# Chunked attention before two layers: heads taken two pairs at a time, one attention cluster in every second slot

## The chip, the cores and the metric

The kernel runs on one core of a Trainium2 chip. The metric is device microseconds of one execution. TensorE (PE) multiplies, VectorE (DVE), ScalarE (ACT) and GpSimd (POOL) do the elementwise work, SyncE (SP) and POOL issue the DMAs. PSUM, where PE writes, is cut here into four tiles of 128x2x512: bank_x, bank_w, bank_y and bank_z.

## The reference, cut to what matters

```python
# q, k, v: (8, 8, 576, 64), in chunks of 64 rows
scores = (1 / np.sqrt(64)) * q_c @ k_c.T              # per head and chunk, 64x64
scores = scores - scores.max(-1, keepdims=True)
attn = np.exp(scores); attn = attn / (attn.sum(-1, keepdims=True) + 1e-9)
x = heads_side_by_side(attn @ v_c)                    # (4608, 512)
h = x @ w_in                                          # 2048 wide
g = np.where(h > 0, h, np.exp(np.minimum(h, 0)) - 1)  # ELU
y = g @ w_out
out = (sigmoid(y @ w_gate) * (y @ w_val)) @ w_out2
```

## The kernel before, in words

Everything is recorded by hand in one order (`manual_schedule`); each engine executes its instructions in that order, and semaphores make it wait for the others. Stage 1 does attention and the first layer, stage 2 the product with w_out, stages 3 and 4 the gated layer and the last product. A large product is three fp32r matmuls ("passes") per pair of 128x128 weights and 512 tokens: high with high, low with high, high with low. So weights and x are split in a high half (a cast on ACT) and a low half (a subtraction on DVE or POOL).

The unit of attention is a pair `A` of heads over 256 tokens, 72 of them. Its steps are `scores` (8 matmuls of 64x64, L463, each two records in the trace), `softmax_max` (DVE, L487 and L488), `softmax_exp` (ACT, L492), `softmax_sum` (DVE L497 and L498; the product L499 on POOL, later on DVE), `transposes` (PE, L505), `transposes_out` (ACT, L514), `values` (8 matmuls, L463) and `values_out` (ACT, L527) into a tile `xr`. When two pairs have filled a tile of 512 tokens, `x_high` (ACT, L380) and `x_low` (DVE, L384) split it. Scores, transposes and values of all pairs lie in bank_x (in `first_steps` in bank_x and bank_z by turns).

The first layer has 72 slots `d`: nine blocks of 512 tokens with eight slots each. A slot's 24 matmuls (`layer_in`, L395) fill one of bank_w, bank_y, bank_z by turns, for two tiles `n` of weights. `elu_exp`, `elu_rest` (ACT, L410, L413) and `elu_sum` (DVE, L418) read that bank in the next slot and store to DRAM. Each slot from 0 to 62 also holds on PE the values of pair d+9, the scores of d+11 and the transposes of d+10, next to one another ahead of the layer's matmuls (in slots 0 to 7 the transposes stand between the halves of the layer).

Before slot 0, `first_steps` takes 11 pairs through the same steps and does parts of the layers of slots 0 and 1. `bg(n)` lets n steps of a background list run: first `convert_in` (w_in from float64 bits; eight units of four steps on ACT, DVE and POOL, 1 MB of load each, two buffers), three steps a slot up to slot 6; then `convert_pairs` for the other weights, about four steps a slot. `join` of unit n issues the load of unit n+2; `rest` of unit n must have run before the layer of slot n.

In stages 3 and 4, `get` and `free` hand out ten buffers; `finish` of a unit multiplies by the gate, stores `s` and `t` to DRAM and frees both.

Of the kernel before, what the change touches and what calls it, by code (L numbers as in the profile page):

```python
# [8 lines left out]
F32 = mybir.dt.float32  # L9
# [16 lines left out]
PB = NPAIR // NB  # L26
KC = DM // 128
# [8 lines left out]
LEAD = 11  # L36
# [3 lines left out]
PRE_STEPS = (0, 0, 0, 1, 1, 1, 1, 1, 1, 1, 1, 2, 2)  # L40
W_AT = (3, 6)
# [19 lines left out]
def kernel(  # L61
# [287 lines left out]
    def shaped(t, shape):  # L349
        n = 1  # L350
        for k in shape:
            n *= k
        names = " ".join("abc"[:len(shape)])
        return t[:, 0:n].rearrange(f"p ({names}) -> p {names}", **dict(zip("abc", shape)))
# [14 lines left out]
    def stage_1():  # L369

        xr, xs, raws, vals, st, h_done = {}, {}, {}, {}, {}, {}

        def xr_tile(j, kk):
            if (j, kk) not in xr:
                xr[j, kk] = x_r.tile([128, TB], F32, tag=f"xr{kk}", name=f"xr{kk}")
            return xr[j, kk]

        def x_high(j, kk):
            x = xs[j, kk] = (x_l, x_r)[j % 2].tile([128, 2, TB], F32R, tag=f"xs{kk}", name=f"xs{kk}")
            nc.scalar.copy(out=x[:, 0], in_=xr[j, kk])  # L380

        def x_low(j, kk):
            x = xs[j, kk]
            nc.vector.tensor_sub(out=x[:, 1], in0=xr.pop((j, kk)), in1=x[:, 0])  # L384
# [46 lines left out]
        with (  # L431
# [5 lines left out]
            def with_eps(t):  # L437
                t = t.rearrange("p (n k) -> p n k", n=4)
                nc.gpsimd.memset(t[:, :, CH:], EPS)
                return t  # L440

            e4 = with_eps(c_p.tile([128, 272], F32, name="e4")[:, 0:4 * (CH + 1)])

            def load_raw(A):
                if A < NPAIR:
                    raws[A] = a_p.tile([128, 2, 4, CH], F32, tag="raw", name="raw", bufs=2)
                    nc.sync.dma_start(out=raws[A], in_=qkv[A][:, 0:512])

            def load_values(A):
                if A < NPAIR:  # L450
                    vals[A] = a_p.tile([128, 4, CH], F32, tag="vals", name="vals", bufs=2)
                    nc.sync.dma_start(out=vals[A], in_=qkv[A][:, 512:768])

            def small(tag):
                return a_p.tile([128, 16], F32, tag=tag, name=tag)[:, 0:4].rearrange("p (n k) -> p n k", k=1)
# [16 lines left out]
            def parts(ps, o):  # L472
                return ps[:, :, o:o + 128].rearrange("p g (i k) -> p i g k", i=2)

            def scores(A, ps):
                r = raws.pop(A)
                st[A, "ps"] = ps
                products(ps, 128, r[:, 0], r[:, 1])
                if A >= LEAD:
                    load_raw(A + 2)  # L480

            def softmax_max(A):
                if A not in st:
                    st[A] = [a_p.tile([128, 4, CH], F32, tag=k, name=k) for k in "sp"] + [e4, None]
                ps, s, m = parts(st.pop((A, "ps")), 128), st[A][0], small("m")
                s, m = (t.rearrange("p (i g) k -> p i g k", g=2) for t in (s, m))
                nc.vector.tensor_reduce(out=m[:, :, :, 0], in_=ps, op=ALU.max, axis=AX.X)  # L487
                nc.vector.tensor_tensor(out=s, in0=ps, in1=m.to_broadcast([128, 2, 2, CH]), op=ALU.subtract)  # L488

            def softmax_exp(A):  # L490
                s, _, e, _ = st[A]
                nc.scalar.activation(out=e[:, :, 0:CH], in_=s, func=ACTF.Exp, scale=SCALE)  # L492

            def softmax_sum(A, eng):
                _, p, e, _ = st[A]
                d = small("d")
                nc.vector.tensor_reduce(out=d[:, :, 0], in_=e, op=ALU.add, axis=AX.X)  # L497
                nc.vector.reciprocal(out=d, in_=d)  # L498
                eng.tensor_tensor(out=p, in0=e[:, :, 0:CH], in1=d.to_broadcast([128, 4, CH]), op=ALU.mult)  # L499

            def transposes(A, ps):
                p = st[A][1]
                st[A, "ps"] = ps
                for i in range(2):
                    nc.tensor.transpose(  # L505
                        ps[:, 0, 256 + 128 * i:384 + 128 * i],
                        p[:, 2 * i:2 * i + 2].rearrange("p n k -> p (n k)"), ident,
                    )

            def transposes_out(A):  # L510
                t = st[A][3]
                if t is None:
                    t = st[A][3] = a_p.tile([128, 4, CH], F32, tag="t", name="t")
                nc.scalar.copy(out=t.rearrange("p n q -> p (n q)"), in_=st.pop((A, "ps"))[:, 0, 256:512])  # L514

            def values(A, ps):
                t = st.pop(A)[3]
                st[A, "ps"] = ps
                products(ps, 0, vals.pop(A), t)
                if A >= LEAD:  # L520
                    load_values(A + 2)

            def values_out(A):
                j, i = divmod(A, PB)
                hp, c = divmod(i, 2)
                x = xr_tile(j, hp)[:, 256 * c:256 * c + 256]
                nc.scalar.copy(  # L527
                    out=x.rearrange("p (i g q) -> p i g q", i=2, g=2), in_=parts(st.pop((A, "ps")), 0),
                )
                return (j, hp) if c == 1 else None  # L530

            def first_steps(load_w):

                for A in range(LEAD):
                    t = w_p.tile([128, 1024], F32, tag="w", name="qkv0")
                    nc.sync.dma_start(out=t[:, 0:512], in_=qkv[A][:, 0:512])
                    nc.sync.dma_start(out=t[:, 512:768], in_=qkv[A][:, 512:768])
                    t = t[:, 0:768].rearrange("p (m n k) -> p m n k", m=3, n=4)
                    raws[A], vals[A] = t[:, 0:2], t[:, 2]
                    if A in W_AT:  # L540
                        load_w(W_AT.index(A))
                for A in range(LEAD):
                    t = w_p.tile([128, 1024], F32, tag="w", name="work")
                    s, p = (t[:, o:o + 256].rearrange("p (n k) -> p n k", n=4) for o in (0, 256))
                    st[A] = [s, p, with_eps(t[:, 512:772]), s]
                for A in (LEAD, LEAD + 1):
                    load_raw(A)
                    load_values(A)
                lows = []
                for k in range(PB + 5):  # L550
                    ps = bank["xz"[k % 2]]
                    n = k - 3
                    if 0 <= n < LEAD - 1:
                        transposes(n, ps)
                    if k < LEAD:
                        scores(k, ps)
                    n = k - 4
                    if 0 <= n < PB + 1:
                        values(n, ps)
                    for d in range(EARLY):  # L560
                        if 2 * d + 1 in w1:
                            layer_in(d, min((k - 5) // 2, KC))
                    for x in lows:
                        x_low(*x)
                    lows = []
                    if 0 <= k - 1 < LEAD:
                        softmax_exp(k - 1)
                    if 0 <= k - 2 < LEAD:
                        softmax_sum(k - 2, nc.gpsimd)
                    steps = PRE_STEPS[k] if k < len(PRE_STEPS) else 0  # L570
                    bg(steps // 2)
                    if k < LEAD:
                        softmax_max(k)
                    if 0 <= k - 3 < LEAD - 1:
                        transposes_out(k - 3)
                    if 0 <= k - 4 < PB + 1:
                        x = values_out(k - 4)
                        if x is not None:
                            x_high(*x)
                            lows.append(x)  # L580
                    bg((steps + 1) // 2)
                for x in lows:
                    x_low(*x)

            def slot(d, steps):

                c = LEAD + d
                ps = bank["x"]
                q = [steps // 3 + (i < steps % 3) for i in range(3)]
                if c - 2 < NPAIR:  # L590
                    values(c - 2, ps)
                if c < NPAIR:
                    scores(c, ps)
                if d < HF:
                    layer_in(d, KC, (0,))
                if c - 1 < NPAIR:
                    transposes(c - 1, ps)
                layer_in(d, KC, (1,) if d < HF else (0, 1))
# [487 lines left out]
```

## Time and profile before

| | |
|---|---|
| median of three runs | 1637.91 us (1636.05 to 1639.51) |
| the profiled execution | 1638.73 us, of which the span from first to last instruction is 1636.9 us |
| granted TensorE clock, mean | 0.997 of full speed |
| PE busy | 1602.9 us, 98% of the span |
| DVE, ACT, POOL busy | 1200.1, 749.1, 303.8 us |
| DMA | 423.19 MB, mean 259 GB/s |

Busy times are unions over a stretch; an engine can wait inside an instruction's gap without it being seen in them. In a row of the timeline an entry in brackets is the idle time ahead of the instruction and what ended it. PE's records overlap, since a matmul starts while the one before it drains; the distance between starts is what one costs.

### The profile page before, as it was taken

What the parts mean: (1) busy time and instruction counts of PE and PEld (TensorE: products, weight loads), DVE (VectorE), ACT (ScalarE), POOL (GpSimd) and SP (SyncE); (2) the same over time, 40 slices, a digit from 0 to 9 for tenths busy, and PEclk for the clock granted to TensorE, in tenths of its full rate; (3) what the DMA queues carried; (4) which work ended last, traced back from release to release, by engine and by line L of the source; (5) the groups of instructions that cost most, each with busy time, mean ns of one, the idle gap of its engine ahead of it and who ended that gap; (6) DMA issues with size and microseconds to landing.
All of it is one profiled execution on the core that took longest, in us unless ns stands there. A gap on an engine that the chain in (4) does not pass through costs nothing.

```text
span 1636.9 us, 25299 instructions
## 1 busy us (share of the span) xinstructions
PE 1602.9 (98%) x9636; PEld 1330.7 (81%) x9636; DVE 1200.1 (73%) x1662; ACT 749.1 (46%) x1244; POOL 303.8 (19%) x491
## 2 busy tenths in 40 slices
PE   6899999999999999999999999999999998999999
PEld 4677777777788898888888888888889887888888
DVE  6878888888637679988865676676675446777775
ACT  5767667766644455554442233332332123344342
POOL 3431111112101112222121223212211113000000
PEclk9999999999999999999999999999999999999999
DMA  6668888888887779999699769869565679433331
GB/s 229 206 216 293 296 293 290 278 288 291 280 292 257 224 297 390 378 336 410 210 302 322 251 208 385 303 222 407 180 206 174 216 261 391 180 141 140 144 103 52
DMA packets 157192, 423.19 MB, mean 259 GB/s; under 512 B 13840, under 2 KB 31248, under 8 KB 149904
## 3 DMA queue, kind: packets, MB, share of 16 engines
q0 software_dynamic: 71760, 218.13, 40.0%
q1 hardware_dynamic: 85312, 203.45, 35.7%
q8 instruction: 76, 1.25, 0.3%
q14 instruction: 44, 0.36, 0.1%
HBM read 288.88 MB, written 132.64 MB: 258 GB/s over the span
## 4 chain that ended last, share of the span: by engine, by line
PE 75%; DVE 12%; ACT 8%; issue 2%; DMA 2%; POOL 0%; SPq 0%; ACTq 0%; DVEq 0%; POOLq 0%
PE bank_z L747 11%; PE bank_y L747 11%; PE bank_x L747 10%; PE bank_x L902 9%; PE bank_y L902 9%; PE bank_z L902 9%; PE bank_w L747 5%; PE bank_w L902 5%; DVE elu L418 2%; PE bank_z L395 2%; PE bank_y L395 2%; PE bank_w L395 2%; DVE s L488 1%; ACT elu L413 1%; DVE m L487 1%
## 5 line engine op out<-in xcount | busy, mean ns | idle before, releaser
L95 ACT CAST four<-b 128x512 fp32r<-128x512 f32 (+1 forms) x240 | 128.0, 577 | 79.1 <-PE bank_z L747 20.9
L101 DVE TENSOR_TENSOR four<-b,four 128x512 fp32r<-128x512 f32 (+1 forms) x240 | 140.0, 631 | 30.5 <-ACT four L95 30.4
L902 PE MATMUL bank_z<-four,w 128*128 128x512 f32 (+1 forms) x720 | 157.6, 368 | 0.0
L924 ACT ACTIVATE s<-s 128x512 f32<-128x512 f32 (+1 forms) x60 | 35.4, 590 | 250.0 <-DVE s L104 250.0
L902 PEld LDWEIGHTS bank_z<-four,w 128*128 128x128 f32 x720 | 126.3, 189 | 22.5
L337 POOL DMA_DIRECT2D w<-wd_glu x159 | 86.1, 545 | 301.7 <-PE bank_x L902 115.1
L395 PE MATMUL bank_w<-xs,w 128*128 128x512 f32 x576 | 139.8, 397 | 0.0
L395 PE MATMUL bank_y<-xs,w 128*128 128x512 f32 x576 | 138.1, 394 | 1.4 <-POOL w L167 0.9
L395 PE MATMUL bank_z<-xs,w 128*128 128x512 f32 x576 | 138.8, 397 | 0.0
L395 PEld LDWEIGHTS bank_z<-xs,w 128*128 128x128 f32 x576 | 107.6, 190 | 21.7
L395 PEld LDWEIGHTS bank_y<-xs,w 128*128 128x128 f32 x576 | 106.2, 188 | 23.1 <-POOL w L167 1.2
L395 PEld LDWEIGHTS bank_w<-xs,w 128*128 128x128 f32 x576 | 106.9, 189 | 21.7
L337 POOL DMA_DIRECT2D w<-wd_mid x105 | 56.0, 537 | 265.8 <-PE bank_x L747 83.1
L747 PE MATMUL bank_x<-four,w 128*128 128x512 f32 (+1 forms) x480 | 100.2, 368 | 0.0
L747 PE MATMUL bank_y<-four,w 128*128 128x512 f32 (+1 forms) x480 | 100.2, 368 | 0.0
L747 PE MATMUL bank_z<-four,w 128*128 128x512 f32 (+1 forms) x480 | 100.2, 368 | 0.0
L747 PEld LDWEIGHTS bank_x<-four,w 128*128 128x128 f32 x480 | 83.7, 189 | 15.0
L747 PEld LDWEIGHTS bank_y<-four,w 128*128 128x128 f32 x480 | 83.7, 189 | 15.0
L747 PEld LDWEIGHTS bank_z<-four,w 128*128 128x128 f32 x480 | 83.7, 189 | 15.0
L104 DVE TENSOR_TENSOR s<-bank_z,s 128x1024 f32<-128x1024 f32 (+1 forms) x60 | 66.9, 1115 | 36.2 <-PE bank_z L902 35.1
L902 PE MATMUL bank_y<-four,w 128*128 128x512 f32 (+1 forms) x432 | 88.5, 354 | 0.1
L902 PE MATMUL bank_x<-four,w 128*128 128x512 f32 (+1 forms) x432 | 88.4, 354 | 0.0
(145 smaller groups left out, 3144.0 us busy)
## 6 DMA issues: line engine op xcount, KB each, us to landing
w<-wd_glu POOLq DMA_DIRECT2D x159, 512.0 KB, 7.9
w<-wd_mid POOLq DMA_DIRECT2D x105, 512.0 KB, 8.2
gd<-elu SPq DMA_DIRECT2D x72, 512.0 KB, 3.9
b<-gd SPq DMA_DIRECT2D x32, 1024.0 KB, 9.0
wd_glu<-ch POOLq DMA_DIRECT2D x36, 512.0 KB, 5.1
b<-gv SPq DMA_DIRECT2D x16, 1024.0 KB, 5.2
raw<-in_qkv SPq DMA_DIRECT2D x61, 256.0 KB, 4.0
wd_mid<-ch POOLq DMA_DIRECT2D x24, 512.0 KB, 5.0
```

Of the source, the lines that this page charges most:

```text
L95: nc.scalar.copy(out=out, in_=raw)
L101: lo_eng.tensor_sub(out=lo, in0=raw, in1=hi)
L104: nc.vector.tensor_tensor(out=out, in0=a, in1=b, op=ALU.add)
L337: nc.gpsimd.dma_start(out=t, in_=wd[m][q][:, LEFT[i]])
L395: nc.tensor.matmul(out=h_bank(d)[:, n], lhsT=w[:, zw, kk * 128:(kk + 1) * 128], rhs=xs[j, kk][:, zx], start=(kk == 0 and p == 0), stop=(kk ...
L413: nc.scalar.activation(out=elu[d], in_=elu[d], func=ACTF.Relu, scale=-1.0, bias=1.0)
L418: nc.vector.scalar_tensor_tensor(out=e, in0=h_bank(d), scalar=0.0, in1=e, op0=ALU.max, op1=ALU.subtract,)
L487: nc.vector.tensor_reduce(out=m[:, :, :, 0], in_=ps, op=ALU.max, axis=AX.X)
L488: nc.vector.tensor_tensor(out=s, in0=ps, in1=m.to_broadcast([128, 2, 2, CH]), op=ALU.subtract)
L747: nc.tensor.matmul(out=bank[PRODUCTS[i]][:, u, 0:NLS[j]], lhsT=w[:, k, zw, 128 * u:128 * u + 128], rhs=t[k][:, zx], start=(i < 4 and p == ...
L902: nc.tensor.matmul(out=ps[:, b], lhsT=w[:, b, zw, 128 * k:128 * k + 128], rhs=x_part(j, i, zx, k), start=(i < 4 and k == 0 and p == 0), st ...
L924: nc.scalar.activation(out=x, in_=x if of is None else of, func=ACTF.Sigmoid)
```

## The change

The unit becomes a group `G` of two pairs (36 of them), and `LEAD` goes from 11 pairs to 6 groups. Softmax instructions take eight heads' chunks (128x512) in place of four (128x256), a group's two exp tiles are shared by all groups, and p is written over s. A slot with even d holds the values of group d/2+4, the scores of d/2+6 and the transposes of d/2+5, between the two halves of the layer; a slot with odd d holds only its layer on PE, and `softmax_sum` on DVE. The transposes go to the second half of the bank that the next slot's layer will sum in (`h_bank(d + 1)[:, 1]`), so they wait for `elu_sum(d - 2)`, and the layer of slot d+1 waits for `transposes_out`. `values_out` and `xr` are gone: `x_high` and `x_low` read bank_x. `elu_rest` follows `elu_exp` at once. `first_steps` has six iterations and twelve background steps as before; each now waits for its own exp. In stage 4 the two buffers of the last unit are freed three products later.

```diff
-LEAD = 11
+LEAD = 6
-PRE_STEPS = (0, 0, 0, 1, 1, 1, 1, 1, 1, 1, 1, 2, 2)
+PRE_STEPS = (0, 1, 2, 3, 3, 3)
+        def x_high(j, kk, ps):
+            xs[j, kk] = (x_l, x_r)[j % 2].tile([128, 2, TB], F32R, tag=f"xs{kk}", name=f"xs{kk}")
+            nc.scalar.copy(out=half(j, kk, 0), in_=parts(ps, 0))
+        def x_low(j, kk, ps):
+            nc.vector.tensor_sub(out=half(j, kk, 1), in0=parts(ps, 0), in1=half(j, kk, 0))
...
+                for k in range(LEAD):
+                    scores(k, own(k))
+                    if k >= 2:
+                        values(k - 2, own(k))
+                    if k >= 1:
+                        transposes(k - 1, own(k - 1)[:, :, 256:512])
...
+                layer_in(d, KC, (0,))
+                if even:
+                    if G - 2 < NG:
+                        values(G - 2, ps)
+                    if G < NG:
+                        scores(G, ps)
+                    if G - 1 < NG:
+                        transposes(G - 1, (
+                            own(G - 1)[:, :, 256:512] if d == 0 else
+                            h_bank(d + 1)[:, 1].rearrange("p (g n) -> p g n", g=2)
+                        ))
+                layer_in(d, KC, (1,))
                 if d > 0:
                     elu_exp(d - 1)
+                    elu_rest(d - 1)
                 bg(q[0])
+                if even:
+                    if d > 0:
+                        elu_sum(d - 1)
+                    if G < NG:
+                        softmax_max(G)
+                    if G - 1 < NG:
+                        transposes_out(G - 1)
+                    if G - 2 < NG:
+                        x_high(*x_of(G - 2), ps)
+                    if G < NG:
+                        softmax_exp(G)
+                    bg(q[1])
+                    if G - 2 < NG:
+                        x_low(*x_of(G - 2), ps)
+                else:
+                    if G < NG:
+                        softmax_sum(G, nc.gpsimd if d < HF - 1 else nc.vector)
                     elu_sum(d - 1)
+                    bg(q[1])
...
-                    while pending:
-                        pending.pop(0)()
+                    if pending:
+                        done = pending.pop(0)()
+                    elif j == i == 0 and p == QO - 1:
+                        for x in done:
+                            free(x)
```

PE in slot 9 of before, from the cluster to the next one (bank_w is this slot's layer, the xs tiles are block 1's four quarters of x):

```order
L463 MATMUL bank_x<-t,vals 64x64 x8
L463 MATMUL bank_x<-raw 64x64 x8
L505 MATMUL bank_x<-ident,p 128x128 x2
L395 MATMUL bank_w<-xs_625,w 128x512 x3
L395 MATMUL bank_w<-xs_760,w 128x512 x3
L395 MATMUL bank_w<-xs_912,w 128x512 x3
L395 MATMUL bank_w<-xs_1063,w 128x512 x3
L395 MATMUL bank_w<-xs_625,w 128x512 x3
L395 MATMUL bank_w<-xs_760,w 128x512 x3
L395 MATMUL bank_w<-xs_912,w 128x512 x3
L395 MATMUL bank_w<-xs_1063,w 128x512 x3
L463 MATMUL bank_x<-t,vals 64x64 x8
```

PE in slot 8 of the changed kernel and the start of slot 9 (bank_z is slot 8's layer, bank_w slot 9's):

```order
L396 MATMUL bank_z<-xs_557,w 128x512 x3
L396 MATMUL bank_z<-xs_669,w 128x512 x3
L396 MATMUL bank_z<-xs_808,w 128x512 x3
L396 MATMUL bank_z<-xs_936,w 128x512 x3
L473 MATMUL bank_x<-t,vals 64x64 x16
L473 MATMUL bank_x<-raw 64x64 x16
L513 MATMUL bank_w<-ident,s 128x128 x4
L396 MATMUL bank_z<-xs_557,w 128x512 x3
L396 MATMUL bank_z<-xs_669,w 128x512 x3
L396 MATMUL bank_z<-xs_808,w 128x512 x3
L396 MATMUL bank_z<-xs_936,w 128x512 x3
L396 MATMUL bank_w<-xs_557,w 128x512 x3
```

The cluster is twice as large, comes once in 48 layer matmuls in place of once in 24, and its transposes stand in bank_w, which slot 9's layer fills next.

DVE at the start of stage 4 of before, with the waits (t_12499 is `t2`, the first difference that the last product needs; s and t above it are the last unit's gate products):

```order
L977 TENSOR_TENSOR s<-s 128x2x256 [waits Activation_49]
L979 TENSOR_TENSOR t<-t 128x256
L720 TENSOR_TENSOR t_12499<-b_12196,b_12009 128x2048 [waits DMAHW6_49,DMAHW2_49,Pool_49]
L101 TENSOR_TENSOR gc<-t_12499,gc 128x2x512 [waits DMAHW3_49,Activation_49]
L101 TENSOR_TENSOR gc<-t_12499,gc 128x2x512 [waits Activation_49]
```

The same place in the changed kernel:

```order
L978 TENSOR_TENSOR s<-s 128x2x256 [waits Activation_49]
L980 TENSOR_TENSOR t<-t 128x256
L720 TENSOR_TENSOR t_11827<-b_11524,b_11337 128x2048 [waits DMAHW6_49,DMAHW2_49,Pool_49]
L102 TENSOR_TENSOR gc<-t_11827,gc 128x2x512 [waits DMAHW7_49,Activation_49]
L102 TENSOR_TENSOR gc<-t_11827,gc 128x2x512 [waits Activation_49]
```

Nothing moved here: `t2` still takes a buffer that a product of POOL's unit left, and waits for POOL and for stores.

## Rows read from the trace of the kernel before

**Rows 1.** Busy time of each engine, by stretch.

```profile
core 0: us, PE busy (x) PEld busy (x) DVE busy (x) ACT busy (x) POOL busy (x), PEclk, DMA share, GB/s
0.00:25.40 25.40, 12.47 (x236) 8.64 (x236) 15.30 (x35) 12.36 (x25) 6.50 (x26) 1.00 0.89 306
25.40:53.50 28.10, 20.34 (x256) 14.20 (x252) 23.42 (x40) 18.81 (x37) 13.93 (x12) 1.00 0.35 122
53.50:98.00 44.50, 41.75 (x358) 32.40 (x351) 34.53 (x52) 31.31 (x50) 19.35 (x20) 0.96 0.63 210
98.00:460.00 362.00, 359.83 (x3148) 286.98 (x3148) 302.33 (x588) 241.77 (x438) 70.53 (x106) 1.00 0.87 284
```

**Rows 2.** What PE waited for, whole span.

```profile
PE bank_x L463 <- ACT xr L527: 5.3, 4, 2.9
PE bank_w L747 <- ACT gc L95: 4.0, 1, 4.0
PE bank_x L505 <- DVE p L499: 2.2, 9, 0.7
```

**Rows 3.** Timeline of PE: a slot of stage 1, then a slot without attention.

```profile
203.00 5.73 PE L395 MATMUL bank_w<-xs,w 128*128 128x512 f32 x24
208.66 0.46 PE L463 MATMUL bank_x<-t,vals 64*64 64x64 f32 x16
208.94 0.41 PE L463 MATMUL bank_x<-raw 64*64 64x64 f32 x16
209.28 0.44 PE L505 MATMUL bank_x<-ident,p 128*128 128x128 f32 x2
209.48 5.70 PE L395 MATMUL bank_y<-xs,w 128*128 128x512 f32 x24
...
465.46 5.60 PE L395 MATMUL bank_z<-xs,w 128*128 128x512 f32 x24
470.90 5.60 PE L395 MATMUL bank_w<-xs,w 128*128 128x512 f32 x24
```

**Rows 4.** Timeline of PE: first matmuls of the layers of slots 8, 60, 64.

```profile
98.02 0.71 PE L395 MATMUL bank_z<-xs,w 128*128 128x512 f32 x2
436.76 0.48 PE L395 MATMUL bank_w<-xs,w 128*128 128x512 f32 x1
460.02 0.61 PE L395 MATMUL bank_y<-xs,w 128*128 128x512 f32 x2
```

**Rows 5.** Groups by line: elementwise instructions of attention, and two of 128x1024.

```profile
L104 DVE TENSOR_TENSOR s<-bank_z,s 128x1024 f32<-128x1024 f32 (+1 forms) x60 | 66.9, 1115 | 36.2 <-PE bank_z L902 35.1
L101 DVE TENSOR_TENSOR gc<-b,gc 128x1024 fp32r<-128x1024 f32 (+1 forms) x60 | 64.3, 1112 | 15.7 <-ACT gc L95 15.7
L463 PE MATMUL bank_x<-raw 64*64 64x64 f32 x976 | 25.2, 218 | 0.0
L505 PE MATMUL bank_x<-ident,p 128*128 128x128 f32 x122 | 26.4, 298 | 2.7 <-DVE p L499 2.2 <-POOL p L499 0.5
L488 DVE TENSOR_TENSOR s<-bank_x,m 128x256 f32<-128x256 f32 x61 | 25.9, 424 | 2.1
L498 DVE RECIPROCAL d<-d 128x4 f32<-128x4 f32 x72 | 12.8, 178 | 2.5
L527 ACT COPY xr<-bank_x 128x256 f32<-128x256 f32 x68 | 25.7, 378 | 0.0
L413 ACT ACTIVATE elu<-elu 128x1024 f32<-128x1024 f32 x72 | 76.3, 1060 | 0.3
```

**Rows 6.** Timeline of PE around the layer of slot 2.

```profile
52.91 0.46 PE L463 MATMUL bank_x<-t,vals 64*64 64x64 f32 x16 [2.92 <-ACT xr L527]
...
53.54 4.61 PE L395 MATMUL bank_z<-xs,w 128*128 128x512 f32 x12
```

**Rows 7.** Timeline at the start of stage 4: DVE and PE.

```profile
1374.98 2.29 DVE L720 TENSOR_TENSOR t<-b,b 128x2048 f32<-128x2048 f32 x1 [4.26 <-issue]
1379.27 1.22 PE L747 MATMUL bank_w<-gc,w 128*128 128x512 f32 x2 [4.04 <-ACT gc L95]
```

More of the change, by code (lines that the diff above doesn't have):

```diff
@@ L369, in stage_1, with parts, half @@
     def stage_1():
[L371 to L384, printed above, removed]
+        xs, raws, vals, st, h_done = {}, {}, {}, {}, {}
+        def parts(ps, o):
+            return ps[:, :, o:o + 256].rearrange("p g (i k) -> p i g k", i=4)
+        def half(j, kk, z):
+            return xs[j, kk][:, z].rearrange("p (i g q) -> p i g q", i=4, g=2)
+        def x_high(j, kk, ps):
[3 more added lines that the diff above has]
+            nc.vector.tensor_sub(out=half(j, kk, 1), in0=parts(ps, 0), in1=half(j, kk, 0))
         def h_bank(d):
@@ L470, in products, with scores @@
                             )
[L472 to L485, printed above, removed]
+            def scores(G, ps):
+                r = raws.pop(G)
+                st[G, "scores"] = ps
+                for a in range(2):
+                    products(ps, 256 + 128 * a, r[:, a, 0], r[:, a, 1])
+                if G >= LEAD:
+                    load_raw(G + 2)
@@ L486, in softmax_max @@
+            def softmax_max(G):
+                if G not in st:
+                    st[G] = [a_p.tile([128, 8, CH], F32, tag=k, name=k) for k in "st"]
+                ps, s, m = parts(st.pop((G, "scores")), 256), st[G][0], small("m")
                 s, m = (t.rearrange("p (i g) k -> p i g k", g=2) for t in (s, m))
                 nc.vector.tensor_reduce(out=m[:, :, :, 0], in_=ps, op=ALU.max, axis=AX.X)
-                nc.vector.tensor_tensor(out=s, in0=ps, in1=m.to_broadcast([128, 2, 2, CH]), op=ALU.subtract)
@@ L497, in softmax_sum @@
+            def softmax_sum(G, eng):
+                e, d = exps[G % 2], small("d")
                 nc.vector.tensor_reduce(out=d[:, :, 0], in_=e, op=ALU.add, axis=AX.X)
                 nc.vector.reciprocal(out=d, in_=d)
[L499 to L504, printed above, removed]
+                eng.tensor_tensor(
+                    out=st[G][0], in0=e[:, :, 0:CH], in1=d.to_broadcast([128, 8, CH]), op=ALU.mult,
+                )
@@ L505, in transposes @@
+            def transposes(G, ps):
+                p = st[G][0]
+                st[G, "turned"] = ps
+                for i in range(4):
                     nc.tensor.transpose(
-                        ps[:, 0, 256 + 128 * i:384 + 128 * i],
+                        ps[:, i // 2, 128 * (i % 2):128 * (i % 2) + 128],
                         p[:, 2 * i:2 * i + 2].rearrange("p n k -> p (n k)"), ident,
                     )
[L510 to L526, printed above, removed]
+            def transposes_out(G):
                 nc.scalar.copy(
[L528 removed]
+                    out=st[G][1].rearrange("p (g n) q -> p g (n q)", g=2), in_=st.pop((G, "turned")),
@@ L529, in values_out @@
                 )
-                return (j, hp) if c == 1 else None
-            def first_steps(load_w):
[L534 to L559, printed above, removed]
@@ new lines, in values, with x_of, own, some @@
+            def values(G, ps):
+                t = st.pop(G)[1]
+                v = vals.pop(G)
+                for a in range(2):
+                    products(ps, 128 * a, v[:, a], t[:, 4 * a:4 * a + 4])
+                if G >= LEAD:
+                    load_values(G + 2)
+            def x_of(G):
+                return divmod(G, KC)
+            def own(G):
+                return bank["xz"[G % 2]]
+            def first_steps(load_w):
+                def some(name, shape):
+                    return shaped(w_p.tile([128, 1024], F32, tag="w", name=name), shape)
+                for G in range(LEAD + 1):
+                    if G < LEAD:
+                        raw_into(some("qkv0", (2, 2, 4, CH)), G)
+                    if G > 0:
+                        if G % 2 == 1:
+                            both = some("qkv0", (2, 2, 4, CH))
+                        values_into(both[:, 1 - G % 2], G - 1)
+                    if G in W_AT:
+                        load_w(W_AT.index(G))
+                for G in range(LEAD):
+                    if G % 2 == 0:
+                        both = some("work", (2, 8, CH))
+                    st[G] = [both[:, G % 2]] * 2
+                for G in (LEAD, LEAD + 1):
+                    load_raw(G)
+                    load_values(G)
+                for k in range(LEAD):
[4 more added lines that the diff above has]
+                        transposes(k - 1, own(k - 1)[:, :, 256:512])
@@ L571, in first_steps @@
[L571 to L583, printed above, removed]
+                            layer_in(d, min(k - 2, KC))
@@ L585, in slot @@
+                    softmax_max(k)
+                    if k >= 2:
+                        x_high(*x_of(k - 2), own(k))
+                    softmax_exp(k)
+                    bg(PRE_STEPS[k] // 2)
+                    if k >= 2:
+                        x_low(*x_of(k - 2), own(k))
+                    softmax_sum(k, nc.gpsimd)
+                    if k >= 1:
+                        transposes_out(k - 1)
+                    bg((PRE_STEPS[k] + 1) // 2)
             def slot(d, steps):
-                c = LEAD + d
+                even, (n, g) = d % 2 == 0, divmod(d, 2)
@@ L588, in slot @@
+                G = LEAD + n
                 ps = bank["x"]
                 q = [steps // 3 + (i < steps % 3) for i in range(3)]
[L590 to L598, printed above, removed]
+                layer_in(d, KC, (0,))
```

84 lines of the change are left out of this document (32 added, 52 removed).

## The prediction

> **What bounds the kernel now.** I read the stretches first, then PE's waits, then PE's timeline. The stretches [rows 1] say where PE is the bound: from 98 us to 460 us it is busy 359.8 of 362.0 us, while DVE is busy 302.3 and ACT 241.8. Ahead of 98 us it is not: PE is busy 74.6 of 98, in 25.4 to 53.5 only 20.3 of 28.1, with DVE at 23.4 of it. After 460 us nothing is edited but one `free`. So there are two stretches with different limits, and each gets its own term. PE's waits [rows 2] name two that the edit touches: 5.3 us for ACT's copy into `xr`, 2.2 us for p. The reader should see that in the second stretch nothing is won by relieving DVE or ACT; only PE's own time counts there. In the first it is the other way round.
>
> **Term 1, slots 8 to 63 (98.02 to 460.02 us).** A layer without attention costs 465.46 to 470.90 = 5.44 us [rows 3]. The stretch between the first matmuls of slots 8 and 64 is 362.0 us [rows 4]; 56 layers are 304.6, so attention costs PE 57.4 us there. An undisturbed slot is 203.00 to 209.48 = 6.48 us, 6.45 in most others, so one cluster costs 1.01. Slots 8 to 59 take 436.76 - 98.02 = 338.7 us, 6.51 each: 52 x 0.06 = 3.3 us of the 57.4 are not work but waits, nearly all for p [rows 2].
>
> After, the small matmuls are all still there; what goes is every second start and end of a cluster. A cluster of twice the size costs the old 1.01 plus 16 values records, 16 scores records and two transposes. For 16 more records: values start at 208.66 and scores at 208.94, 0.28 us with a cluster's start in it; from the first to the last start of the scores it is 0.41 - 0.22 = 0.19 [rows 3, 5]. I take 0.23, between them. For two more transposes: 0.20 (209.28 to the layer at 209.48) at least, 0.60 (two times 298 ns) at most; the two records together span 0.44, so the second starts 0.44 - 0.30 = 0.14 to 0.17 after the first, and I take 0.33. The new cluster is 1.01 + 0.46 + 0.33 = 1.80 us, in place of 2.02 for two old ones. Bounds: 1.59 and 2.17.
>
> From slot 8 there are 26 whole clusters (even slots 8 to 58), one without scores (slot 60: 1.34) and one of values alone (slot 62: some 0.7): 26 x 1.80 + 2.0 = 48.8 us. Term 1 is 57.4 - 48.8 = **8.6 us gained**. With the bounds of the new cluster it lies between 1.3 us lost and 14.3 gained. 3.3 of the 8.6 are the wait for p. It goes because p has a whole odd slot to be made in: `softmax_sum` stands in the odd slot and its transposes come half a slot into the next even one.
>
> What covers the waits that the change adds? The transposes now also wait for `elu_sum(d - 2)`, behind which stand, on PE, half a layer and all that follows. That sum stands in the slot before, behind two or so background steps and `softmax_sum`. With PE's slots of 7.2 (even) and 5.4 us (odd), it has until 2.7 us into the even slot, and ACT's part of it (two activations of 1024 elements, 1.06 us each [rows 5]) is done some 2.4 us into the odd one. DVE has less to do than before: an instruction of 256 elements takes 424 ns and one of 1024 takes 1115 [rows 5], so 512 take about 0.65, and each merged pair saves 0.2; with the second reciprocal (0.18) a group saves some 0.8 us on DVE in 12.7. DVE's share falls from 84% to below 80%. So I cost the wait at nothing. If that cover is gone, it is the second rival below. `x_high` and `x_low` out of PSUM: an addition with an input from PSUM takes 1115 ns, a subtraction from SBUF alone 1112 [rows 5], so I cost the new source at nothing; the copies of 378 ns, 36 x 2 of them, go from ACT, which is not the bound.
>
> [...]
>
> On the queues: SP issues one load of values for each group in place of two, the same bytes; the raw loads stay two. SP's stores behind them wait for the same `elu_sum` as before.
>
> **Term 2, the start (0 to 98 us).** The first matmul of slot 8 stands at 98.02. In this stretch DVE is busy 15.3 + 23.4 + 34.5 = 73.3 us and ACT 62.5 [rows 1]. Some ten groups go through in it. Each saves DVE 0.8 us (as above, p being on POOL here), and saves ACT two copies of 378 ns, and 0.15 to 0.2 on each of exp and the copy of the transposes, about 1.1 us. Ten groups: 8 us of DVE's 73, 11 of ACT's 62. If DVE sets the pace, the 98 us shrink by 8 x 98/73 = 10.7; if its idle time stays as long as it is, by 8. On PE, the 5.3 us of waits for `xr` go [rows 2], since bank_x is now used in every second slot; the longest, 2.92, stands just ahead of slot 2's layer [rows 6]. What is late next is the weights: three steps a slot remain, so the last unit's `rest` still runs in slot 6, and slot 7's layer would wait some 2 us for it, as PE gets there sooner. I take **8 us gained**, the smaller of the two. Bounds: 0, if the weights' conversion sets the pace whatever attention costs; 14, if all of PE's idle time from 25.4 to 98 (72.6 - 62.1 = 10.5 us) goes, with some 3 from a shorter first phase.
>
> The clock shows in a row here: slot 2's first 12 matmuls took 4.61 us [rows 6] at a granted clock that averages 0.96 over 53.5 to 98 [rows 1], after 2.92 us in which PE did nothing; 12 at full clock are half of 5.44 [rows 3], so 1.9 us were lost. I count this as part of the 8.
>
> [...]
>
> **Term 3, the freed buffers.** PE's wait of 4.0 us at the start of stage 4 hangs on `t2`, which began 4.26 us after DVE was free [rows 7]. The order shows `t2` with the same waits as before, for POOL and for stores, so it gets the same buffer: 0. The later buffers that do change are wanted after that wait.
>
> **Sum.** The profiled execution: 1638.73 - 8.6 - 8 = 1622.1 us. It was 0.8 above the median of the runs (1637.91), so I predict **1621.5**.
>
> **The rivals.**
> First, the weights pace the start: `convert_in` keeps its three steps a slot and each unit its chain of load, four DVE steps and POOL's subtraction, so slot 8 begins at 98 as before. For it: POOL and the loads do the same work as before. Against it: DVE and ACT, on which the units also run, get 8 and 11 us free. Only term 1 is left: 1637.9 - 8.6 = 1629.3.
>
> Second, on the other side, the odd slot waits for `transposes_out`. The bank with the transposes is the next slot's, and its layer begins 2.7 us after the cluster. ACT reaches the copy (about 0.6 us) behind `elu_exp`, `elu_rest` and two background steps, some of which wait for DVE. If DVE runs a good 3 us behind, PE waits 1.2 us in each of 28 pairs of slots: 34 us, and the time is 1655. It decides from 16.6/28 = 0.6 us a cluster on. Against it: 2.1 us of slack by the durations, and a DVE below 80%.
>
> Third, the first phase gets slower. Its iterations no longer have three pairs in flight: on one bank scores, maximum, difference, `x_high`, exp, sum, p, transposes and the copy follow each other, about 8 us, and two banks alternate. If they overlap poorly, six iterations and 4 us of first load end near 52 us and not at 43; 9 us lost against 8.6 gained: 1638.
>
> Fourth, the lower clock in the early pieces: 36 matmuls at 0.16 us more each (1.9/12) are 5.8 us: 1627.3.
>
> Fifth, the freed buffers take the wait away after all: 4 us and the slow stretch behind it, 1616. The order speaks against it.
>
> **How the numbers follow.** The likeliest case, both terms, 0.58, with 1614 to 1629 of its own; weights pace the start, 0.16; odd slots wait, 0.07; slower first phase, 0.06; lower clock, 0.08; freed buffers, 0.05. The range of 1612 to 1632 takes in the likeliest case, the weights, the lower clock and the freed buffers, and most of the bounds of term 2; about 0.17 is left out, the two slow cases and the far ends. A measurement of this kernel tells some 0.2% (3.3 us) from no change: faster than 1634.6 has 0.58 + 0.16 + 0.08 + 0.05 = 0.87, slower than 1641.2 the second rival's 0.07, and the third's 0.06 is the middle.
>
> **What would show it.** Two slots from slot 8 on should take 2 x 5.44 + 1.80 = 12.68 us in place of 12.9 to 13.0, with no wait of PE for p; slot 8's first matmul should stand near 90 us, slot 64's near 443.5; PE's wait for `xr` should be gone and one for `rest` of the weights in slot 7 should be longer than now. The 4.0 us at the start of stage 4 should stand as they are. Wrong would be: a PE wait for ACT at each odd slot's first layer matmul; pairs of slots above 12.9 us; slot 8 at 98 or later.

## The result, and the profile after

The changed kernel takes 1618.12 us (median of 4 runs, 1616.59 to 1622.02) against 1638.71 (4 runs); the ratio is 0.988, 95% interval 0.9858 to 0.9902. The profiled execution, the slowest of the four, took 1622.02, 16.7 us less than the one of before. The prediction had 1621.5 for the median and 16.6 us for the profiled execution.

Busy time of each engine by stretch, cut at the first layer matmuls of slots 2, 8 and 64:

```profile
core 0: us, PE busy (x) PEld busy (x) DVE busy (x) ACT busy (x) POOL busy (x), PEclk, DMA share, GB/s
0.00:25.40 25.40, 12.53 (x270) 10.20 (x271) 15.86 (x25) 11.71 (x16) 7.23 (x13) 1.00 0.95 346
25.40:42.42 17.02, 15.03 (x187) 12.15 (x187) 16.62 (x20) 10.31 (x16) 10.41 (x8) 1.00 0.36 127
42.42:92.24 49.82, 42.45 (x349) 33.24 (x349) 40.48 (x44) 33.80 (x43) 21.50 (x18) 0.93 0.59 204
92.24:444.25 352.01, 352.01 (x3182) 288.65 (x3180) 284.37 (x452) 230.17 (x329) 68.75 (x106) 1.00 0.88 290
444.25:1620.00 1175.75, 1167.41 (x5653) 988.16 (x5651) 824.87 (x951) 444.79 (x697) 193.43 (x329) 1.00 0.74 255
```

Against [rows 1, 4]: slots 8 to 63 take 352.0 us, not 362.0, and PE has no idle time left in them. Slot 8's layer begins at 92.24, not 98.02. The rest is 0.9 us shorter. 10.0 + 5.8 + 0.9 is the 16.7. The boundary is the prediction's, the first layer matmul; before, slot 8's cluster stands ahead of it (from 97.20 on), after, behind it, so 0.8 of the 5.8 us are only this. The six slots 2 to 7 answer to 53.54 to 98.02 in [rows 4, 6]: 11.1 us were won up to slot 2 (0.6 of them by the boundary again), and 5.3 given back in those six. Up to slot 2 PE's idle time fell from 20.7 to 14.9 us and its busy time from 32.8 to 27.6.

PE's timeline: an even slot's cluster with the end of the layer's first half ahead of it and the second half behind it, and then the places in slots 2 to 7 where PE waited, with slot 3 (from 54.05), where it did not:

```profile
157.61 0.62 PE L396 MATMUL bank_w<-xs,w 128*128 128x512 f32 x2
158.15 0.70 PE L473 MATMUL bank_x<-t,vals 64*64 64x64 f32 x32
158.67 0.65 PE L473 MATMUL bank_x<-raw 64*64 64x64 f32 x32
159.24 0.66 PE L513 MATMUL bank_y<-ident,s 128*128 128x128 f32 x4
159.66 3.03 PE L396 MATMUL bank_w<-xs,w 128*128 128x512 f32 x12
...
49.24 0.63 PE L513 MATMUL bank_w<-ident,s 128*128 128x128 f32 x4 [2.71 <-DVE elu L419]
49.63 4.58 PE L396 MATMUL bank_z<-xs,w 128*128 128x512 f32 x12
54.05 5.62 PE L396 MATMUL bank_w<-xs,w 128*128 128x512 f32 x24
...
69.48 7.36 PE L396 MATMUL bank_z<-xs,w 128*128 128x512 f32 x24 [2.64 <-ACT t L519]
...
78.15 2.83 PE L396 MATMUL bank_w<-xs,w 128*128 128x512 f32 x11 [1.08 <-POOL w L168]
...
86.85 5.55 PE L396 MATMUL bank_y<-xs,w 128*128 128x512 f32 x23 [0.86 <-POOL w L168]
```

Values, scores and transposes now come in runs of twice as many records [rows 3], but with one way in and one way out. The two waits of over 2.5 us cost more than their length: the 12 matmuls behind the first then take 4.58 us (3.03 in the undisturbed slot above), the 24 behind the second 7.36 (5.62 in slot 3). The granted clock (the figure behind POOL's) shows it, 0.61 over the 12 matmuls behind the first wait, 1.00 in slot 3 and 0.76 in slot 5:

```profile
49.63:54.05 4.42, 4.42 (x16) 3.51 (x15) 4.35 (x4) 3.79 (x5) 1.77 (x2) 0.61 0.84 289
54.05:59.40 5.35, 5.35 (x25) 4.43 (x24) 5.18 (x7) 3.58 (x6) 1.76 (x2) 1.00 0.49 158
69.48:76.69 7.21, 7.21 (x25) 5.76 (x25) 6.96 (x10) 5.99 (x8) 1.31 (x2) 0.76 0.44 166
```

What PE waited for over the whole span, the seven longest. Against [rows 2, 7], the waits for `xr`, all ahead of slot 8, and those for p from slot 8 on are gone, and stage 4's stands in this execution too. In `first_steps` PE still waits, for loads, for ACT's copy of the transposes (L519) and for p (L505).

```profile
PE bank_x L473 <- DMA qkv<-in_qkv: 4.4, 2, 3.5
PE bank_z L473 <- ACT work L519: 4.2, 2, 2.2
PE bank_w L747 <- ACT gc L96: 3.9, 1, 3.9
PE bank_w L513 <- DVE elu L419: 2.7, 1, 2.7
PE bank_x L473 <- ACT work L519: 2.7, 1, 2.7
PE bank_z L396 <- ACT t L519: 2.6, 1, 2.6
PE bank_x L513 <- POOL work L505: 2.6, 2, 2.0
```

### The profile page after: what moved, and what is told of

It is laid out like the page before. It is cut to its first block, busy times and chain, and to the rows that moved or that the text cites. A ratio compares the mean times of both kernels' runs of the same rounds, so it can differ in the third digit from the quotient of the medians.

```text
span 1620.2 us, 24888 instructions
## 1 busy us (share of the span) xinstructions
PE 1589.4 (98%) x9636; PEld 1332.4 (82%) x9636; DVE 1182.2 (73%) x1491; ACT 730.8 (45%) x1100; POOL 301.3 (19%) x472
## 4 chain that ended last, share of the span: by engine, by line
PE 94%; DVE 2%; DMA 2%; ACT 1%; issue 1%; POOL 0%; SPq 0%; DVEq 0%; ACTq 0%
PE bank_z L747 11%; PE bank_y L747 11%; PE bank_x L747 10%; PE bank_x L902 9%; PE bank_z L902 9%; PE bank_y L902 9%; PE bank_z L396 7%; PE bank_y L396 7%; PE bank_w L396 7%; PE bank_w L747 5%; PE bank_w L902 5%; PE bank_x L473 2%; DMA gv<-t 1%; DMA qkv<-in_qkv 0%; DMA raw<-in_qkv 0%
## 5 line engine op out<-in xcount | busy, mean ns | idle before, releaser
L747 PEld LDWEIGHTS bank_z<-four,w 128*128 128x128 f32 x480 | 83.8, 189 | 14.9
L747 PEld LDWEIGHTS bank_y<-four,w 128*128 128x128 f32 x480 | 83.8, 189 | 14.9
```

The source lines that it names most:

```text
L747: nc.tensor.matmul(out=bank[PRODUCTS[i]][:, u, 0:NLS[j]], lhsT=w[:, k, zw, 128 * u:128 * u + 128], rhs=t[k][:, zx], start=(i < 4 and p == ...
```

## The experiments

My theory: PE alone bounds slots 8 to 63, and the gain there is fewer entries into clusters, with p's waits; at the start DVE and ACT set the pace. Rivals: the direct split from PSUM made the gain; the freed buffers did; weights, or the order on ACT, pace the start. Every run had the kernel before beside it on the same chip. S2, S8, S64 are the first layer matmuls of slots 2, 8, 64, in us. In the kernel before, PSUM split alone and transposes apart, slot 8's values and scores stand ahead of S8, in pairs apart half of them (0.6 to 1.1 us); elsewhere they stand behind it. "The second sample" is the run of the changed kernel again.

| run | median us | ratio to before, 95% | S2 | S8 | S64 |
|---|---|---|---|---|---|
| before (profiled at 1638.73) | 1638.71 | | 53.54 | 98.02 | 460.02 |
| changed, again | 1619.30 | 0.9885 to 0.9912 | 42.78 | 92.54 | 444.55 |
| transposes apart | 1621.88 | 0.9899 to 0.9926 | 42.62 | 95.05 | 447.85 |
| pairs apart | 1631.57 | 0.9953 to 0.9981 | 42.58 | 94.31 | 456.43 |
| PSUM split alone | 1687.60 | 1.0290 to 1.0328 | 54.26 | 115.15 | 513.04 |
| copy out first | 1628.52 | 0.9936 to 0.9962 | 42.82 | 95.88 | 454.09 |
| transposes' copy late | 1669.28 | 1.0182 to 1.0210 | 42.96 | 92.25 | 497.11 |
| steps late | 1628.08 | 0.9937 to 0.9965 | 42.42 | 100.98 | 452.99 |
| no clamp | 1618.17 | 0.9876 to 0.9908 | 42.57 | 91.16 | 443.17 |
| low halves on DVE | 1618.42 | 0.9872 to 0.9898 | 43.23 | 92.92 | 444.93 |
| four steps a slot | 1621.40 | 0.9891 to 0.9917 | 42.42 | 94.37 | 446.37 |
| loads first | 1625.11 | 0.9911 to 0.9935 | 50.22 | 96.05 | 448.05 |
| old `free` | 1618.20 | 0.9873 to 0.9898 | 42.53 | 92.27 | 444.27 |

**The changed kernel again.**

> The changed kernel unaltered, for its scatter and as the mate of the others on the same chip. Expected by every theory: 1616 to 1622 us; slot 8's first matmul near 92.2 us, slot 64's near 444.2 (352.0 us between them), even slots 7.18 and odd ones 5.44 us.

As expected: 352.0 us between slots 8 and 64, two slots 12.62. Here the wait at stage 4 does not stand, and the rest after S64 takes 1172.5 us, not 1176.0. No variant below but old `free` and PSUM split alone differs from the changed kernel in stage 4, and of all their profiles only that of pairs apart has this wait (3.8 us; 1.3 at most in the others): it is a matter of the execution.

**What a second cluster costs.** Transposes apart (from slot 8 on; odd slots unchanged):

```
-  layer_in(d, KC, (0,)); values(...); scores(...); transposes(...)
+  values(...); scores(...); layer_in(d, KC, (0,)); transposes(...)
```

> From slot 8 on the values and scores stand ahead of the first half of the layer in every second slot and the transposes between its halves: two clusters where the changed kernel has one, the same matmuls, the same banks. Theory (a cluster's start and end cost PE by themselves): from 1.01 us for a cluster of one pair and 1.74 for one of two, a start and end cost 2 x 1.01 - 1.74 = 0.28 us; the even slot goes from 7.18 to about 7.46, slot 64 comes about 28 x 0.28 = 7.5 us later, and the time is 6 to 9 us above the changed kernel's. Rival (the gain in slots 8 to 63 came from vanished waits and from DVE's and ACT's relief, and the number of clusters costs nothing): even slot 7.18 to 7.22, the time within 2 us of the changed kernel's.

Two slots: 12.69 us (slots 10 to 12: 107.74 to 120.43), 0.07 more than 12.62, near the rival's; the time, 2.6 us more, is a little outside the rival's 2. So my sentence "a start and end costs 0.28" was wrong as it stood. PE's timeline of this run shows why:

```profile
156.65 0.84 PE L396 MATMUL bank_z<-xs,w 128*128 128x512 f32 x3
157.42 0.69 PE L473 MATMUL bank_x<-t,vals 64*64 64x64 f32 x32
157.94 0.65 PE L473 MATMUL bank_x<-raw 64*64 64x64 f32 x32
158.51 3.02 PE L396 MATMUL bank_w<-xs,w 128*128 128x512 f32 x12
161.37 0.60 PE L513 MATMUL bank_y<-ident,s 128*128 128x128 f32 x4
161.73 1.64 PE L396 MATMUL bank_w<-xs,w 128*128 128x512 f32 x6
```

The transposes come in and go out in 161.73 - 161.37 = 0.36 us; in the whole cluster they had 0.42 (159.24 to 159.66) behind the scores. Only the products of 64 rows were still entered once. Hence pairs apart, where both clusters hold products:

```
+  values(..., (0,)); scores(..., (0,))      # first pair
   layer_in(d, KC, (0,))
-  values(...); scores(...); transposes(...)
+  values(..., (1,)); scores(..., (1,)); transposes(...)
```

> From slot 8 on the first pair's values and scores stand ahead of the first half of the layer in every second slot, the second pair's and all four transposes between its halves: two clusters that both hold products, where the two clusters of the run before were products in one and transposes alone in the other. Theory (what costs PE is each change from the layer to the products of 64 rows and back: the holes of about 0.32 - 0.23, 0.05 and 0.15 us in the records around them): 0.2 to 0.3 us in each even slot, 7.38 to 7.48, 5 to 8 us in all, 1624 to 1628. Rival (a second cluster costs 0.07 whatever is in it, as with the transposes alone): 7.25, 2 us, 1621 to 1623.

13.01 us for two slots (slots 10 to 12: 107.32 to 120.33), 0.39 more than the changed kernel; over 27 even slots 10.4 of the some 12 us lost. PE's timeline of such a slot:

```profile
158.72 0.46 PE L473 MATMUL bank_x<-t,vals 64*64 64x64 f32 x16
159.00 0.41 PE L473 MATMUL bank_x<-raw 64*64 64x64 f32 x16
159.34 3.02 PE L396 MATMUL bank_w<-xs,w 128*128 128x512 f32 x12
162.29 0.46 PE L473 MATMUL bank_x<-t,vals 64*64 64x64 f32 x16
```

The theory holds in the narrower form, and its size was too small: an entry into the products and the way back cost 0.39 us, a second cluster of transposes alone 0.07. The 0.39 is more than the merge itself saved: two undisturbed slots took 2 x 6.45 = 12.90 us before, 0.28 more than 12.62. Before, each cluster left by way of its transposes; here the first goes from the scores straight into the layer, whose 12 matmuls take 162.29 - 159.34 = 2.95 us, where half a layer is 2.72. Whether this is the 0.1 us between the two prices no run shows.

**The direct split.** Alone, in the kernel before (`x_high` and `x_low` take halves of 256 elements from `bank_x`, `values_out` is gone):

```
-  nc.scalar.copy(out=x.rearrange(...), in_=parts(..., 0))
+  x_high(j, hp, c, ps)     # x_low from ps follows elu_sum
```

> The kernel before with one part of the change alone: each pair's values are split straight from PSUM, by halves of 256 elements, with no copy to a tile of its own first. Theory (PE bounds slots 8 to 63, the start hangs on DVE and ACT): 362 us between slots 8 and 64 stay within 1 us, since p's waits stay; at the start PE's wait for the copy goes, 0 to 4 us won; time 1634 to 1639. Rival A (the relief of ACT and DVE made most of the change's gain): 1630 or less. Rival B (PE now waits in each slot for DVE's subtraction, where it waited for ACT's copy): 0.1 to 0.3 us in each of 56 slots, 1643 to 1655.

Rival B, at several times its price: 398 us between slots 8 and 64, and 17 us at the start; the granted clock over the whole run was 0.989, 0.997 in the profile of before. PE's row, and the two of DVE that it hangs on:

```profile
164.88 0.46 PE L462 MATMUL bank_x<-t,vals 64*64 64x64 f32 x16 [1.88 <-ACT elu L409]
```

```profile
163.23 1.22 DVE L417 SCALAR_TENSOR_TENSOR elu<-bank_y,elu 128x1024 f32<-128x1024 f32 x1
164.37 0.41 DVE L383 TENSOR_TENSOR xs<-bank_x,xs 128x256 fp32r<-128x256 f32 x1
```

The row names ACT, but `x_low` ends at 164.78 and the values begin 0.1 us later: bank_x is held until DVE has come past the ELU's sum, and every slot wants it. The opposite, pairs by two with the copy kept:

```
+  nc.scalar.copy(out=t.rearrange(...), in_=parts(ps, 0))
-  nc.scalar.copy(out=half(j, kk, 0), in_=parts(ps, 0))
+  nc.scalar.copy(out=xs[j, kk][:, 0], in_=t)
```

> The changed kernel, with each group's values copied out of PSUM by ACT first and split from that copy, as the kernel before did; the pairs by two and the clusters stay. Theory (from slot 8 on PE is the bound and bank_x has a whole odd slot to come free, so the direct split is worth nothing there; at the start it spares ACT some 0.6 us in each group): 12.62 us for two slots as in the changed kernel, slot 8 0 to 3 us later, time 1617 to 1623. Rival (the direct split made a good part of the gain): 12.7 us or more for two slots, time 1626 or more.

The rival holds: about half of the gain is gone, 3.3 us of it at the start, all in slots 2 to 7, and 6.2 between slots 8 and 64 (358.2). PE there:

```profile
200.53 0.65 PE L475 MATMUL bank_x<-raw 64*64 64x64 f32 x32
201.98 0.66 PE L515 MATMUL bank_y<-ident,s 128*128 128x128 f32 x4 [0.81 <-DVE elu L421]
```

The transposes wait for the sum of the ELU two slots back, longest in every third even slot, after an odd one in which four conversion instructions stood ahead on ACT. In the changed kernel this sum ends 1.5 us or more before the transposes in every even slot from 8 to 60; with the copy back that margin shrinks from group to group and is at most 0.06 us in two of every three even slots from 18 to 56. So it is not one copy's 0.6 us but a delay that adds up. The two parts need each other: pairs by two give the bank time, and the direct split gives ACT time.

**The margin of the odd slots.** The prediction's second rival, brought about by moving one copy, from slot 8 on:

```
   softmax_max(G)
-  transposes_out(G - 1)
   x_high(*x_of(G - 2), ps); softmax_exp(G); bg(q[1])
+  transposes_out(G - 1)
```

> From slot 8 on ACT's copy of the transposes stands behind the split's high half, the exponential and the next background steps of its slot, in place of ahead of them: the prediction's second rival made on purpose. In the changed kernel the copy ends some 1.8 us before the odd slot's layer needs its bank. Theory (that margin is all that keeps the odd slots clean): the copy ends 1.5 to 3 us after the bank is wanted, PE waits for it at the first layer matmul of nearly every odd slot, 40 to 80 us in all, 1660 to 1700. Rival (ACT, below 70% busy, makes it up elsewhere): less than 0.5 us in an odd slot, under 1632.

As the theory said: 52.9 us more between slots 8 and 64, for instance

```profile
101.90 1.65 PE L396 MATMUL bank_w<-xs,w 128*128 128x512 f32 x3 [2.32 <-ACT t L519]
```

PE waits for the copy in every odd slot up to 59, and behind the one shown the matmuls are slower too: the 24 of slot 9 take 7.1 us (101.90 to 108.99), 5.44 in the changed kernel. The rival was a real one, kept off by the place of one copy. In the changed kernel the copy ends 2.0 us before the odd slot's layer begins, in every pair of slots.

**The start.** Five edits: the first third of the steps behind the ELU and the softmax in slots 0 to 7; the clamp left out, which does less than the kernel has to; the low halves on DVE; four steps a slot; and the first loads of weights sooner, with two more steps in `first_steps`.

```
   elu_exp(d - 1); elu_rest(d - 1)
-  bg(q[0])
   ...elu_sum, softmax_max, transposes_out, x_high, softmax_exp...
+  bg(q[0])
   bg(q[1])
```

> The changed kernel, with the first third of the weights' steps of slots 0 to 7 moved behind the ELU's and the softmax's work of its slot on ACT and DVE. Theory (in slots 2 to 7 PE waits because the weights' steps stand ahead of the ELU's exponential and the copy of the transposes on ACT): the six slots take 40 to 45 us where they took 49.8, slot 8 begins at 83 to 88 us, and the time is 4 to 9 us below the changed kernel's. Rival (DVE's and POOL's work for the weights sets the pace, whatever the order): slot 8 begins at 91 to 95 us, PE's waits move to POOL's subtraction for the weights of slots 6 and 7, and the time is within 3 us of the changed kernel's.

My theory fell, and the rival's pace did not stay either: slot 8 8.4 us later. PE now waits for weights:

```profile
PE bank_w L396 <- ACT w L160: 4.7, 1, 4.7
```

Its slot 5 waited as long as in the changed kernel, but here the matmuls behind the wait ran at nearly full pace, 24 in 5.73 us (5.62 in slot 3 of the changed kernel), so a wait of this length did not slow them every time:

```profile
72.05 5.73 PE L396 MATMUL bank_z<-xs,w 128*128 128x512 f32 x24 [2.63 <-ACT t L519]
```

```
-  queue((low, n), (clamp, n), (rest, n - 1))
+  queue((low, n), (rest, n - 1))
```

> The changed kernel without the clamp of the eight units of weights that are converted for the first layer (this leaves a part of the conversion out): one DVE instruction of 1024 elements less for each, eight in all, 0.7 to 1.7 us each. Theory (DVE's work sets the pace of the start): slot 8's first matmul comes 4 to 8 us earlier, at 84 to 88 us, time 1611 to 1616. Rival (loads, ACT and POOL set it): less than 2 us, slot 8 at 90.5 or later, 1617 to 1620.

The rival: slot 8 only 1.4 us sooner and slot 2 where it was, though DVE was busy 9.5 us less up to 92.5 us. Busy times, of the second sample and of this run:

```profile
0.00:92.50 92.50, 70.14 (x804) 55.82 (x805) 73.38 (x88) 55.81 (x74) 38.41 (x37) 0.96 0.65 228
0.00:92.50 92.50, 71.54 (x810) 56.80 (x811) 63.89 (x80) 56.79 (x76) 37.85 (x37) 0.91 0.66 233
```

The lower mean clock of this run, 0.91, comes from ahead of slot 2: 0.86 from 0 to 25.4 us and 0.91 from there to 42.5, where the second sample has 1.00 in both.

```
-  nc.gpsimd.tensor_sub(out=w[:, 1], ...)
+  nc.vector.tensor_sub(out=w[:, 1], ...)
```

> The changed kernel with the sixteen subtractions of the first layer's weights (their low halves) on DVE in place of POOL: some 0.7 us each on DVE in place of 1.5 each on POOL. Theory A (POOL's instruction stretches DVE's beside it, 0.68 to 1.25 and more, so that DVE pays for it anyway): slot 8 within 2 us of the changed kernel's 92.4, time within 2 us. Theory B (DVE's own work is all that counts): 11 us more on DVE, slot 8 at 97 to 101 us, time 5 to 9 us more. Theory C (the chain of conversion is what is late, and POOL is its slowest link): slot 8 at 86 to 90 us, time 2 to 6 us less.

Theory A: 0.4 us later. Groups by line, 0 to 93 us, first of the changed kernel (second sample), then of this run:

```profile
L168 POOL TENSOR_TENSOR w<-t,w 128x512 fp32r<-128x512 f32 x16 | 23.4, 1485 | 17.8 <-ACT w L160 17.8
L144 DVE TENSOR_SCALAR t<-t 128x1024 uint32<-128x1024 uint32 x8 | 10.6, 1331 | 0.1
```

```profile
L168 DVE TENSOR_TENSOR w<-t,w 128x512 fp32r<-128x512 f32 x16 | 11.2, 738 | 0.3
L144 DVE TENSOR_SCALAR t<-t 128x1024 uint32<-128x1024 uint32 x8 | 5.5, 684 | 0.0
```

DVE got 11.2 us more to do and was busy only 2.7 longer up to 92.5 us (76.1 against 73.4): with POOL's subtractions gone, its shift took 684 ns, not 1331. One by one, in the first profile of the changed kernel: two of the eight shifts ran with POOL idle and took 0.68 us each; of the six beside POOL's subtractions five took 1.42 to 1.68 and one, at 41.51 us, 0.74.

```
-  IN_STEPS = 3
+  IN_STEPS = 4
```

> The changed kernel with four conversion steps in each of the first slots in place of three, so that the weights are ready sooner and attention's and the ELU's work of slots 0 to 5 comes later. Theory (late weights are what the start hangs on, as moving the steps back by a third of a slot had cost 8 us): slot 8 at 86 to 90 us, time 1612 to 1617. Rival (in slots 2 to 5 the ELU's and the transposes' copy wait behind the steps): slot 8 at 93 to 97, time 1619 to 1624.

The rival: slots 6 and 7 run clean, but slot 2's transposes wait 4.0 us for p.

```
-  PRE_STEPS = (0, 1, 2, 3, 3, 3);  W_AT = (1, 3)
+  PRE_STEPS = (0, 2, 3, 3, 3, 3);  W_AT = (0, 2)
```

> The changed kernel with the loads of the first two units of weights one group earlier in SP's queue, and two more conversion steps in the first iterations. Theory (loads of weights and the chain behind them set the start): slot 2's first matmul at 41 to 44 us, slot 8 at 86 to 90, time 1611 to 1617. Rival (the first iterations get slower by what the weights gain, as queries, keys and values land later): slot 2 at 45 to 48, slot 8 at 92 to 96, time 1618 to 1623.

The rival, with more than its loss: slots 2 to 7 take 45.8 us, 3.9 less than the second sample's 49.8, but slot 2 begins 7.4 us later, behind waits for queries, keys and values (9.2 us up to slot 2, 4.2 in the second sample) and for ACT's copy of the transposes (10.0 against 7.8).

**The freed buffers.** Undone alone: `finish` frees both itself again.

```
-            return s, t
+            free(s)
+            free(t)
```

> The changed kernel with the buffers of the last gated unit freed where the kernel before freed them: one part undone. Theory (the freed buffers are worth nothing): median 1617 to 1621 with runs on both sides of 1620, as the changed kernel has. Rival (they are why some executions have no wait for the split of gc of 3.9 us at the start of stage 4): the wait stands in the profile, and all runs are at 1621 or above.

The theory: the same time, and no wait of 3.9 us at the start of stage 4 in this profile, with the old order. The runs "on both sides of 1620" did not come: its four lie between 1617.9 and 1619.0.

No variant beats the changed kernel by more than its scatter (1616.6 to 1622.4 in eight runs).

## Why the prediction was right

- **Term 1** (8.6 forecast, 10.0 measured): the mechanism was right, the cluster a little cheaper: 7.18 - 5.44 = 1.74 us, not 1.80, and 26 x 0.06 = 1.6 is the difference of 1.4 but for rounding. The working had it from the shared start and end; pairs apart shows these (0.39 us), transposes apart that only the products have them. Some 7 of the 10.0 us are the merge (26 x 0.28), most of the rest are slots that p disturbed. The working's 3.3 us, "nearly all for p", are more than its row: the waits listed there are 2.2.
- **The cover costed at nothing** (the copies "go from ACT, which is not the bound"): the sum was right, the reason too short. Put back, the copy costs 6.2 us in the steady slots. ACT's time as such had no price; the wait for `elu_sum` that it brings on did. The margin of 2.1 us for the odd slots was right (2.0 measured), and as thin as it looked. DVE was relieved by less than worked out: an instruction of 512 elements takes 692 ns, not 650, and DVE's share fell to 81% (284.4 of 352.0 us), not below 80%.
- **The source in PSUM**: costing it at nothing was right. `x_low` takes 692 ns from PSUM after (slots 8 to 63) and 680 from SBUF before, but copy out first, which reads SBUF in the changed kernel, has 692 too, so not even these 12 ns are the source. The kernel before, the changed one and copy out first, slots 8 to 63:

```profile
L384 DVE TENSOR_TENSOR xs<-xr,xs 128x512 fp32r<-128x512 f32 x28 | 19.1, 680 | 0.0
L385 DVE TENSOR_TENSOR xs<-bank_x,xs 128x512 fp32r<-128x512 f32 x28 | 19.4, 692 | 3.2 <-ACT xs L382 2.3
L387 DVE TENSOR_TENSOR xs<-xr,xs 128x512 fp32r<-128x512 f32 x28 | 19.4, 692 | 21.2 <-ACT xs L384 21.2
```

- **Term 2** (8 forecast, 5.8 measured): within its bounds, but not as worked out: the 8 us were spread over the 98, and what came was 11.1 won ahead of slot 2 and 5.3 lost behind it. "What is late next is the weights ... slot 7's layer would wait some 2 us" named a wait that came at 1.08 us in slot 6 and 0.86 in slot 7; slot 7 had waited 0.55 and 0.86 before, so the sign that this wait would grow did not come. The larger two were not in the sum: slot 2's transposes for the first ELU sum (2.71) and slot 5's layer for the copy of the transposes (2.64), the second rival's place for once, each with 1.6 to 1.7 us lost at a lower clock behind it (0.61 and 0.76). And DVE's busy time, from which the 8 us came, does not set the pace: 9.5 us less of it was worth 1.4, 2.7 more cost 0.4. Moving steps either way only trades waits for weights against waits for attention. Nor is the direct split what won the 11.1: with the copy back slot 2 stands at 42.82, and with the split alone in the kernel before at 54.26. That leaves the groups of two pairs and the new order of `first_steps`, which no run separates. Which link holds the start is not settled: in the chain of waits of the second sample, 40 to 93 us, the loads of weights and of queries and keys have 9.9% and 9.4%, no line more than 10.5%.
- **Term 3** (0): right; the old `free` gives the same time.
- **The sum**: 1.4 more from term 1, 2.2 less from term 2 and 0.9 after slot 64 cancel, so that 16.7 against 16.6 is luck. (1622.1 less 0.8 is also 1621.3, not 1621.5.) The profiled execution has stage 4's wait of 3.94 us and is the slowest of its four, which is probably most of why the median fell by 20.6 us and the profile by 16.7; the other executions have no profile to show it. The second sample gives 17.2 (1636.47 for the kernel before beside it).
- **The rivals**: weights pacing the start, the slower first phase and the freed buffers did not come; a lower clock came behind two waits, not in the early pieces, the 36 layer matmuls from 25.69 to 38.00 us: the first 12 took 3.24 us, the next 24 5.58 (32.42 to 38.00), at a granted clock of 1.00. Where the clock was lower ahead of slot 2 (no clamp: 0.86 up to 25.4 us, 0.91 from there to 42.5), slot 2 came no later (42.57).

## What to carry to other kernels

Price a merge by the kind of transition that it removes (here 0.39 us for the products of 64 rows, 0.07 for transposes alone), read from the records on both sides of the hole, not by a flat "start and end". When an operand is read straight from a bank, ask which instruction frees that bank and what is queued ahead of it: the same edit cost 51 us where the bank was wanted every slot and was worth about 10 us where it was wanted every second. Engine time off the bound was not free where an in-order queue put it ahead of something that the bound waits for: one copy a group on ACT cost 6.2 us between slots 8 and 64, a small delay in each group that added up before it showed.

## What had not been expected of the hardware

With POOL's subtractions beside it DVE's shift took nearly twice as long (a mean of 1331 ns against 684), so work moved from POOL to DVE cost DVE a quarter of its length here (2.7 of 11.2 us). Going between the layer's matmuls and transposes cost PE 0.07 us a time, going to the products of 64 rows and back 0.39. In the changed kernel a subtraction of 512 elements took 692 ns whether it read PSUM or, with the copy out first, SBUF. Behind a wait of 2.6 us ahead of slot 5's layer 24 matmuls took 7.36 us in the changed kernel and 5.73 with the steps late.
